# The first batch's softmax divided after the value product: sums from products with ones, in a fused attention and two-FFN kernel

## The chip, the cores and the metric

The kernel runs on one core of a Trainium2 chip. The metric is the device time of one execution in microseconds (us); lower is better. Inputs and outputs are float32 in the chip's main memory.

## What is computed

Three layers, one after the other:

```
attn:  4 batches, 8 heads, 576 positions, 64 columns a head
       scores = q k^T / 8, masked; heads 0-3: a local window (0 <= rel < 32),
       heads 4-7: positions with the same remainder by 32, causal
       e = exp(scores - max);  attn = e / (sum(e) + 1e-9);  out = attn v
x = out as [2304 tokens, 512]
moe:   xn = x / sqrt(mean(x*x) + 1e-6) * rms_g
       y = (silu(xn w_gate) * (xn w_val)) w_out        (512 -> 1536 -> 512)
moe2:  the same without the norm, with weights of its own
```

## The kernel before

**Numbers.** A product of the FFN layers is done on values split into a high and a low part (type fp32r), as three products. The weights are split on the chip: per half megabyte of weights a `weight_step` (line 311) has `low` and `high` on ScalarE (L288, L280), `sign` and `join` on VectorE (L292, L297), then a cast on ScalarE (L305) and a subtraction on VectorE (L309). The products of the attention are plain float32.

**Stages.** Attention is cut into batches. The first batch (`b` = 0) runs alone, ahead of all FFN work (`state["start"]` is true, lines 1134 to 1143); beside it only the first weights are loaded and split. When the first columns of `x` are normed (L887), they are split (L1000, L1001) and the products of the first FFN layer begin. Batches 1 to 3 run in the gaps of that layer. From about a fifth of the run on only FFN work is left.

**One batch** has ten groups: five of strided heads (tiles of 126 or 108 rows) and five of local heads (tiles of 128 queries by 96 keys; the last has half as many). A group has four (the last two) score tiles and goes through three steps, each a list of phases:

- `softmax_step` (line 663): `pe`, the score products on TensorE into one or two banks of PSUM; `top`, on VectorE the mask, the scale and the row minimum (L677); `exp`, on ScalarE one exponential a tile, which also accumulates the row's sum (L686, `accum_out`; the profile shows each as an ACTIVATE and an ACTIVATION_READ_ACCUMULATOR); `norm`, on VectorE sum + 1e-9 and a reciprocal of one column a tile (L696, L697), on GpSimd one multiplication of the group's tiles (L703).
- `turn_step` (line 712): four transposes on TensorE, one copy out of PSUM on ScalarE (`pT`).
- `local_v` / `strided_v` (lines 754, 799): the product with v into a bank `op` of 512 columns, of which 256 or fewer are used, and copies from there into `x` (L87 on ScalarE; in the first two strided groups also a piece of 36 columns on VectorE, L89).

After groups 4, 6 and 9 `squares` (line 828) adds up x squared; `rms_step` (line 849) makes the norm's factor and applies it.

**Order.** `point()` moves every active step on by one phase and starts at most one new one; the list made by `batch` (line 903) puts group i's scores before the transposes of group i-3 and the value product of group i-4. TensorE's order in the first batch is fixed by that list (`traced`, line 53). On the other engines a planner orders what is ready, attention ahead of weight work (`PRIO_W`). Seven banks of PSUM go round among the first batch's steps; the eighth takes the constant products.

**Constant products.** In the first batch `keep_busy` (line 67) puts products of a constant 128x128 by 128x256 (`att.warm`, L72), whose result nobody reads, ahead of chosen groups of products; the number of each place is in a table.

Of the kernel before, what the change touches and what calls it, by code (L numbers as in the profile page):

```python
# [15 lines left out]
DRAM = bass.MemoryType.DRAM  # L16

NEG = -8.0e9
PRIO = 200
PRIO_A = 400  # L20
PRIO_R = 1500
# [4 lines left out]
def attn_ffn_ffn(ctx: ExitStack, tc: tile.TileContext, q, k, v, w1g, w1v, w1o, rms_g, w2g, w2v, w2o, out):  # L26
# [40 lines left out]
    def keep_busy():  # L67
        if state["start"] and state["kind"] and state["group"] != state["filled"]:
            state["filled"] = state["group"]
            state["count"] += 1  # L70
            for _ in range({1: 26, 11: 34, 14: 16, 20: 6, 27: 8, 28: 5, 31: 7, 34: 9, 36: 22, 40: 2, 43: 5}.get(state["count"], 0)):
                traced(nc.tensor.matmul(att.fill, att.warm[:, :128], att.warm, start=True, stop=True))  # L72

    def product(out_, a, b_, start, stop, **how):
# [420 lines left out]
    class Attention:  # L495
        def __init__(self, actx):
            cp = actx.enter_context(tc.tile_pool(name="cp", bufs=1))
            self.p1 = actx.enter_context(tc.tile_pool(name="p1", bufs=1))
            self.p2 = actx.enter_context(tc.tile_pool(name="p2", bufs=2))
            self.ident = cp.tile([128, 128], F32, name="ident")  # L500
            self.ones = cp.tile([128, 128], F32, name="ones")
            self.warm = cp.tile([128, 256], F32R, name="warm")
            self.fill = bank("v")[:, :256]
            self.m0 = cp.tile([128, 96], F32, name="m0")
            self.m1 = cp.tile([128, 96], F32, name="m1")
            self.ms = cp.tile([128, 128], F32, name="ms")[:, 0:126]
            self.gcol = cp.tile([128, 32], F32, name="gcol")[:, 0:KC]
            self.expo = cp.tile([128, 32], F32, name="expo")
            self.ld = {}
            self.vt = {}  # L510
            self.qk = {}
            self.st = {}
            self.x = {}
            self.ss = {}
            self.done = set()
            self.sq = set()
            self.turned = {}
            self.nbank = 0
            self.tags = ["a0", "a1", "g", "y0", "y1", "y2", "y3"]
            self.turn = 0  # L520
# [10 lines left out]
        def consts(self):  # L531
            g = nc.gpsimd

            def sel(t, pattern, base, cm, op=ALU.is_ge, fill=NEG):
                g.affine_select(out=t, in_=t, pattern=pattern, compare_op=op, fill=fill, base=base, channel_multiplier=cm)

            row = self.ms[0:7]
            g.memset(row, 0.0)
            sel(row[:, 0:108].rearrange("p (t a) -> p t a", a=6), [[0, 18], [-1, 6]], 0, 1, ALU.not_equal, 1.0)
            sel(row[:, 108:126], [[0, 18]], -6, 1, ALU.not_equal, 1.0)  # L540
            same = bank("g")
            nc.tensor.matmul(same[0:126, 0:126], row, row, start=True, stop=True)
            nc.vector.tensor_scalar(out=self.ms[0:126], in0=same[0:126, 0:126], scalar1=1.0, scalar2=-NEG, op0=ALU.subtract, op1=ALU.mult)
            for m, leads in ((self.m0, (0, 32)), (self.m1, (32, 32))):
                g.memset(m, 0.0)
                for par, lead in enumerate(leads):
                    sel(m[64 * par:64 * par + 64], [[-1, 96]], lead, 1)
                    sel(m[64 * par:64 * par + 64], [[1, 96]], 31 - lead, -1)
            sel(self.ms[0:126], [[-1, 126]], 0, 1)
            g.memset(self.expo, -0.5)  # L550
            nc.sync.dma_start(out=self.gcol, in_=rms_g.rearrange("(c p) -> p c", p=128))

        def load_strided(self, t, src, b, eng):
# [109 lines left out]
        def softmax_step(self, ready, key, qn, kn, mks, mms):  # L663

            cell = {}
            nt = len(mks)

            def pe():
                cell["s"] = mms()

            def top():
                sp = cell["s"]
                cell["e"] = e = self.p2.tile([128, 4, 128], F32, tag="e", name="e", bufs=6)
                cell["nb"] = nb = self.p2.tile([128, 32], F32, tag="nb", name="nb", bufs=6)
                for i, mk in sorted(enumerate(mks), key=lambda im: im[0] % 2):

                    r = nc.vector.tensor_tensor_reduce(out=e[:qn, i, :kn], in0=sp[i], in1=mk[:qn, :kn], scale=-0.125,  # L677
                                                       scalar=3.0e38, op0=ALU.add, op1=ALU.min, accum_out=nb[:qn, i:i + 1])
                if state["start"]:
                    last["dve"] = ins_of(r)  # L680

            def exp():
                e, nb = cell["e"], cell["nb"]
                cell["sums"] = sums = self.p2.tile([128, 32], F32, tag="sums", name="sums", bufs=6)
                for i in range(nt):
                    r = nc.scalar.activation(out=e[:qn, i, :kn], in_=e[:qn, i, :kn], func=AF.Exp, bias=nb[:qn, i:i + 1],  # L686
                                             scale=-1.0, accum_out=sums[:qn, i:i + 1])
                if state["start"]:
                    last["act"] = ins_of(r)

            def norm():
                e, sums = cell["e"], cell["sums"]
                rc = self.p2.tile([128, 32], F32, tag="rc", name="rc", bufs=6)
                self.nnorm = getattr(self, "nnorm", -1) + 1
                eng = nc.gpsimd
                nc.vector.tensor_scalar(out=sums[:qn, :nt], in0=sums[:qn, :nt], scalar1=1e-9, scalar2=None, op0=ALU.add)  # L696
                nc.vector.reciprocal(out=rc[:qn, :nt], in_=sums[:qn, :nt])  # L697
                if eng is None:
                    for i in range(nt):
                        nc.vector.tensor_scalar(out=e[:qn, i, :kn], in0=e[:qn, i, :kn], scalar1=rc[:qn, i:i + 1], scalar2=None,  # L700
                                                op0=ALU.mult)
                if eng is not None:
                    eng.tensor_tensor(out=e[:qn, :nt, :kn], in0=e[:qn, :nt, :kn], in1=rc[:qn, :nt].unsqueeze(2).to_broadcast([qn, nt, kn]), op=ALU.mult)  # L703
                if key[1] == 0 or not 3:
                    self.st[key] = e

            def put():
                self.st[key] = cell["e"]

            return Step([pe, top, exp, norm] + ([wait] * (3 - 1) + [put] if 3 and key[1] else []), ready, kind="s")  # L710

        def turn_step(self, key, qn, kn, nt):
            cell = {}
# [40 lines left out]
        def local_v(self, b, tiles, last):  # L754
            cell = {}

            def pe():
                cell["o"] = op = self.abank()
                vt = self.vt[b, 0]
                pT = self.st.pop(("T", ("l", b, tiles)))  # L760
                n = 0
                for i, halves in enumerate(tiles):
                    for par, (pair, j) in enumerate(halves):
                        for hp in range(2):
                            product(op[64 * hp:64 * hp + 64, 64 * n:64 * n + 64], vt[:, 2 * pair + hp, j, :],
                                    pT[:96, 2 * i + hp, 64 * par:64 * par + 64], start=True, stop=True)
                        n += 1

            def post():
                x = self.x_tile(b, 0)  # L770
                p0, j0 = tiles[0][0]
                if j0 == NW - 1:
                    copy(self.eng(), x[:, :, 64 * j0:S], cell["o"][:, 0:128].rearrange("p (a k) -> p a k", a=2))
                else:
                    copy(self.eng(), x[:, p0, 64 * j0:64 * (j0 + 4)], cell["o"][:, 0:256])

            return Step([pe, post] + ([lambda: self.squares(b, last)] if last else []),
                        lambda: ("T", ("l", b, tiles)) in self.st, kind="v")
# [20 lines left out]
        def strided_v(self, b, part, pair):  # L799
# [4 lines left out]
            def pe():  # L804
# [3 lines left out]
                for k in range(2):  # L808
                    for hp in range(2):
                        i = 2 * k + hp if pair is None else 2 * hp + k  # L810
                        gi, h = subs[i]
                        g = 2 * part + gi
                        product(op[64 * hp:64 * hp + 64, 128 * k:128 * k + n], vt[:n, h, g * D:(g + 1) * D], pT[:n, i, :n], start=True, stop=True)

            def post():
                x = self.x_tile(b, 1)
                for k in range(2):
                    g = 2 * part + k if pair is not None else 4
                    d = x[:, k if pair is None else pair].rearrange("p (t r) -> p t r", r=32)
# [908 lines left out]
```

## Time and profile before

| | |
|---|---|
| median of 3 runs | 997.48 us (997.15 to 999.68) |
| profiled execution, own time | 1001.4 us |
| its span | 999.5 us |
| busy: TensorE / weight loads / VectorE / ScalarE / GpSimd | 969.5 / 892.3 / 582.3 / 577.7 / 385.3 us |
| mean granted TensorE clock | 0.995 |

The busy shares are averages over stages that differ. The change touches the first batch alone, the stretch up to about 52 us; after 70 us TensorE is busy nearly all the time. So what counts is how long the opening takes and what the engines still owe when it ends.

### The profile page before, as it was taken

Reading aid. Unit: us, or ns where it says so; the run is one execution under the profiler, and the core shown is the slowest. Engines: PE = TensorE matmul, PEld = TensorE weight load, DVE = VectorE, ACT = ScalarE, POOL = GpSimd, SP = SyncE. Lnnn points to the kernel's source line nnn. Section 1 sums busy time; section 2 is a strip of 40 time slices with the busy share of each in tenths; the row PEclk is TensorE's granted clock in tenths of the full one; section 3 lists DMA queues with packets and bytes.
Section 4 is the critical chain, followed back from the end, with each engine's and each line's share of the span. In section 5 each row is a group of like instructions: output and inputs, shape, how many; then the busy total and the mean of one; then the engine's idle time right before and its main releaser. Section 6 shows DMA issues by size and latency. Waiting matters only on the chain.

```text
span 999.5 us, 17788 instructions
## 1 busy us (share of the span) xinstructions
PE 969.5 (97%) x6054; PEld 892.3 (89%) x6054; DVE 582.3 (58%) x1319; ACT 577.7 (58%) x1465; POOL 385.3 (39%) x416
## 2 busy tenths in 40 slices
PE   8889998999999999999999999999999999999998
PEld 8778866777989999899999998999999999899997
DVE  5796768867335656456645646545557554563334
ACT  6998776864335645456554556554656546553431
POOL 3221244621221628152535556571616334341500
PEclk9999999999999999999999999999999999999999
DMA  7884558848684766996758685556978396865211
GB/s 195 230 218 149 155 176 255 260 161 304 208 293 153 216 195 196 317 297 205 248 190 288 238 261 209 177 199 250 316 263 260 117 348 218 292 208 164 88 61 64
DMA packets 168455, 215.89 MB, mean 216 GB/s; under 512 B 46860, under 2 KB 122028, under 8 KB 168364
## 3 DMA queue, kind: packets, MB, share of 16 engines
q1 hardware_dynamic: 158559, 199.48, 61.8%
q10 hardware_dynamic: 9805, 15.27, 4.2%
q8 instruction: 48, 0.79, 0.3%
q14 instruction: 43, 0.35, 0.1%
HBM read 142.87 MB, written 71.83 MB: 215 GB/s over the span
## 4 chain that ended last, share of the span: by engine, by line
PE 79%; DMA 8%; ACT 6%; DVE 4%; issue 2%; SPq 1%; POOL 0%; ACTq 0%; DVEq 0%; POOLq 0%
PE b_y L76 33%; PE b_a L76 17%; PE b_g L76 14%; PE b_v L76 13%; DMA raw<-in_moe_w_out_dram 2%; PE b_y L80 2%; DMA pk<-raw 1%; ACT e L686 1%; DMA part<-ob 1%; PE b_a L80 1%; SPq L160 1%; ACT raw L288 1%; ACT dh L280 1%; DVE dh L297 1%; DMA ob<-part 1%
## 5 line engine op out<-in xcount | busy, mean ns | idle before, releaser
L1401 POOL TENSOR_TENSOR xl<-xst,xh 128x384 fp32r<-128x384 f32 x196 | 210.7, 1096 | 181.5 <-ACT xh L1400 61.8
L76 PE MATMUL b_y<-xh,w 128*128 128x384 f32 (+1 forms) x800 | 215.3, 334 | 2.5 <-ACT t L1458 2.1
L76 PEld LDWEIGHTS b_y<-xh,w 128*128 128x128 f32 x800 | 145.7, 188 | 5.5 <-ACT t L1458 2.7
L76 PE MATMUL b_a<-xh,w 128*128 128x384 f32 (+2 forms) x512 | 141.6, 336 | 3.0 <-ACT t L1458 3.0
L76 PE MATMUL b_y<-xl,w 128*128 128x384 f32 (+1 forms) x400 | 133.6, 334 | 0.0
L76 PE MATMUL b_g<-xh,w 128*128 128x384 f32 (+2 forms) x408 | 125.6, 349 | 0.3 <-DVE w L309 0.3
L76 PE MATMUL b_v<-xh,w 128*128 128x384 f32 (+2 forms) x344 | 105.9, 351 | 1.3 <-ACT t L1472 1.3
L76 PEld LDWEIGHTS b_a<-xh,w 128*128 128x128 f32 x512 | 93.2, 188 | 7.0 <-ACT t L1458 4.7
L1400 ACT CAST xh<-xst 128x384 fp32r<-128x384 f32 x196 | 91.6, 520 | 0.0
L386 POOL TENSOR_TENSOR raw<-dh 128x256 f32<-128x256 f32 x40 | 29.6, 757 | 153.1 <-DVE dh L297 55.5
L76 PE MATMUL b_a<-xl,w 128*128 128x384 f32 (+2 forms) x256 | 85.9, 335 | 0.0
L76 PE MATMUL b_y<-hh,w 128*128 128x384 f32 (+2 forms) x304 | 81.2, 341 | 0.0
L76 PEld LDWEIGHTS b_g<-xh,w 128*128 128x128 f32 x408 | 75.5, 190 | 5.7 <-DVE w L309 0.5
L76 PEld LDWEIGHTS b_y<-xl,w 128*128 128x128 f32 x400 | 75.1, 188 | 1.8
L76 PEld LDWEIGHTS b_v<-xh,w 128*128 128x128 f32 x344 | 63.6, 190 | 6.6 <-ACT t L1472 1.6
L76 PE MATMUL b_g<-xl,w 128*128 128x384 f32 (+2 forms) x204 | 69.2, 339 | 0.0
L703 POOL TENSOR_TENSOR e<-e,rc 128x384 f32<-128x384 f32 (+3 forms) x40 | 37.1, 932 | 79.1 <-DVE rc L697 19.8
L76 PE MATMUL b_y<-w,hh 128*128 128x512 f32 x216 | 67.1, 391 | 0.0
L686 ACT ACTIVATE e<-e,nb 128x96 f32<-128x96 f32 (+2 forms) x152 | 57.1, 382 | 4.6 <-DVE nb L677 4.3
L76 PE MATMUL b_v<-xl,w 128*128 128x384 f32 (+2 forms) x172 | 58.7, 341 | 0.0
L76 PEld LDWEIGHTS b_y<-hh,w 128*128 128x128 f32 x304 | 54.8, 188 | 3.1 <-issue 0.2
L1478 DVE TENSOR_TENSOR b_y<-b_y,t 128x384 f32<-128x384 f32 x56 | 31.7, 566 | 42.4 <-ACT b_y L1472 41.5
(216 smaller groups left out, 2152.8 us busy)
## 6 DMA issues: line engine op xcount, KB each, us to landing
w<-pk SPq DMA_DIRECT2D x48, 512.0 KB
raw<-in_moe_w_gate_dram SPq DMA_DIRECT2D x24, 512.0 KB
raw<-in_moe_w_val_dram SPq DMA_DIRECT2D x24, 512.0 KB
raw<-in_moe_w_out_dram SPq DMA_DIRECT2D x24, 512.0 KB
pk<-raw ACTq DMA_DIRECT2D x48, 256.0 KB
part<-ob SPq DMA_DIRECT2D x48, 256.0 KB
xst<-y_d SPq DMA_DIRECT2D x30, 384.0 KB
xst<-xq SPq DMA_DIRECT2D x28, 384.0 KB
```

Source lines behind the costliest of these rows:

```text
L76: traced(nc.tensor.matmul(out_, a, b_, start=start, stop=stop, **how))
L80: traced(nc.tensor.transpose(out_, a, one))
L160: nc.sync.dma_start(out=out, in_=in_)
L280: nc.scalar.activation(out=cell["h"], in_=cell["hw"].bitcast(F32), func=AF.Copy, scale=2.0 ** -112)
L288: nc.scalar.activation(out=cell["r"], in_=cell["lw"], func=AF.Copy, scale=LOW)
L297: nc.vector.scalar_tensor_tensor(out=h, in0=h, scalar=3, in1=cell["r"], op0=ALU.logical_shift_left, op1=ALU.bitwise_or)
L386: paced(nc.gpsimd.tensor_tensor(out=t[:, z], in0=a, in1=b, op=ALU.subtract))
L686: r = nc.scalar.activation(out=e[:qn, i, :kn], in_=e[:qn, i, :kn], func=AF.Exp, bias=nb[:qn, i:i + 1], scale=-1.0, accum_out=sums[:qn, i:i ...
L703: eng.tensor_tensor(out=e[:qn, :nt, :kn], in0=e[:qn, :nt, :kn], in1=rc[:qn, :nt].unsqueeze(2).to_broadcast([qn, nt, kn]), op=ALU.mult)
L1400: nc.scalar.copy(out=xh[:, kk], in_=src[:, kk])
L1401: paced(nc.gpsimd.tensor_tensor(out=xl[:, kk], in0=src[:, kk], in1=xh[:, kk].bitcast(F32), op=ALU.subtract), ("pe", None))
L1478: nc.vector.tensor_tensor(out=s, in0=s, in1=v, op=ALU.mult)
```

## The change

In the first batch, and there alone (`key[1]` or `b` is 0):

- The exponentials don't accumulate sums, and the `norm` phase is gone: raw exponentials are transposed and multiplied with v.
- After the value product of a group, `sums_of` writes the row sums into the other half of the same bank: one product of three constant rows (`tiny` by `warm`, which gives the 1e-9) and, for each of the two halves of the partitions, one float32 product of ones with the group's transposed tiles (256 columns; 252 or 216 in strided groups; half in the last group).
- `inverse` takes, on VectorE, the reciprocal of those sums (all of them: each query has its sum in 64 partitions) into a tile of `e`; then VectorE multiplies the value product by it on the way into `x`, in place of ScalarE's copies: one multiplication in a local group, two in a strided one, three in the first two.
- The table of constant products has 54 fewer, of 114 that come after the first one's 26.
- Three small GpSimd instructions and one VectorE copy make `tiny` at the start.

```diff
@@ -16,6 +16,7 @@
 DRAM = bass.MemoryType.DRAM
 
 NEG = -8.0e9
+EPS = (137 * 2.0 ** -37, 56 * 2.0 ** -44, 95 * 2.0 ** -53)
 PRIO = 200
 PRIO_A = 400
 PRIO_R = 1500
@@ -68,7 +69,7 @@
         if state["start"] and state["kind"] and state["group"] != state["filled"]:
             state["filled"] = state["group"]
             state["count"] += 1
-            for _ in range({1: 26, 11: 34, 14: 16, 20: 6, 27: 8, 28: 5, 31: 7, 34: 9, 36: 22, 40: 2, 43: 5}.get(state["count"], 0)):
+            for _ in range({1: 26, 11: 20, 14: 10, 20: 3, 27: 4, 28: 2, 31: 3, 34: 4, 36: 8, 40: 1, 43: 5}.get(state["count"], 0)):
                 traced(nc.tensor.matmul(att.fill, att.warm[:, :128], att.warm, start=True, stop=True))
 
     def product(out_, a, b_, start, stop, **how):
@@ -505,6 +506,7 @@
             self.m1 = cp.tile([128, 96], F32, name="m1")
             self.ms = cp.tile([128, 128], F32, name="ms")[:, 0:126]
             self.gcol = cp.tile([128, 32], F32, name="gcol")[:, 0:KC]
+            self.tiny = cp.tile([128, 128], F32R, name="tiny")[0:3]
             self.expo = cp.tile([128, 32], F32, name="expo")
             self.ld = {}
             self.vt = {}
@@ -548,6 +550,11 @@
                     sel(m[64 * par:64 * par + 64], [[1, 96]], 31 - lead, -1)
             sel(self.ms[0:126], [[-1, 126]], 0, 1)
             g.memset(self.expo, -0.5)
+            eps = self.p2.tile([128, 32], F32, tag="nb", name="eps", bufs=6)[0:3]
+            g.memset(eps, EPS[0])
+            sel(eps, [[0, 32]], 0, -1, fill=EPS[1])
+            sel(eps, [[0, 32]], 1, -1, fill=EPS[2])
+            nc.vector.tensor_copy(out=self.tiny.rearrange("p (a k) -> p a k", a=4), in_=eps.unsqueeze(1).to_broadcast([3, 4, 32]))
             nc.sync.dma_start(out=self.gcol, in_=rms_g.rearrange("(c p) -> p c", p=128))
 
         def load_strided(self, t, src, b, eng):
@@ -681,33 +688,42 @@
 
             def exp():
                 e, nb = cell["e"], cell["nb"]
+                if not key[1]:
+                    for i in range(nt):
+                        r = nc.scalar.activation(out=e[:qn, i, :kn], in_=e[:qn, i, :kn], func=AF.Exp, bias=nb[:qn, i:i + 1], scale=-1.0)
+                    last["act"] = ins_of(r)
+                    self.st[key] = e
+                    return
                 cell["sums"] = sums = self.p2.tile([128, 32], F32, tag="sums", name="sums", bufs=6)
                 for i in range(nt):
-                    r = nc.scalar.activation(out=e[:qn, i, :kn], in_=e[:qn, i, :kn], func=AF.Exp, bias=nb[:qn, i:i + 1],
-                                             scale=-1.0, accum_out=sums[:qn, i:i + 1])
-                if state["start"]:
-                    last["act"] = ins_of(r)
+                    nc.scalar.activation(out=e[:qn, i, :kn], in_=e[:qn, i, :kn], func=AF.Exp, bias=nb[:qn, i:i + 1],
+                                         scale=-1.0, accum_out=sums[:qn, i:i + 1])
 
             def norm():
                 e, sums = cell["e"], cell["sums"]
                 rc = self.p2.tile([128, 32], F32, tag="rc", name="rc", bufs=6)
-                self.nnorm = getattr(self, "nnorm", -1) + 1
-                eng = nc.gpsimd
                 nc.vector.tensor_scalar(out=sums[:qn, :nt], in0=sums[:qn, :nt], scalar1=1e-9, scalar2=None, op0=ALU.add)
                 nc.vector.reciprocal(out=rc[:qn, :nt], in_=sums[:qn, :nt])
-                if eng is None:
-                    for i in range(nt):
-                        nc.vector.tensor_scalar(out=e[:qn, i, :kn], in0=e[:qn, i, :kn], scalar1=rc[:qn, i:i + 1], scalar2=None,
-                                                op0=ALU.mult)
-                if eng is not None:
-                    eng.tensor_tensor(out=e[:qn, :nt, :kn], in0=e[:qn, :nt, :kn], in1=rc[:qn, :nt].unsqueeze(2).to_broadcast([qn, nt, kn]), op=ALU.mult)
-                if key[1] == 0 or not 3:
-                    self.st[key] = e
+                nc.gpsimd.tensor_tensor(out=e[:qn, :nt, :kn], in0=e[:qn, :nt, :kn], in1=rc[:qn, :nt].unsqueeze(2).to_broadcast([qn, nt, kn]), op=ALU.mult)
 
             def put():
                 self.st[key] = cell["e"]
 
-            return Step([pe, top, exp, norm] + ([wait] * (3 - 1) + [put] if 3 and key[1] else []), ready, kind="s")
+            return Step([pe, top, exp] + ([norm, wait, wait, put] if key[1] else []), ready, kind="s")
+
+        def sums_of(self, out_, n, parts_):
+
+            k, w = parts_[0].shape[1:]
+            out_ = out_.rearrange("p (k m) -> p k m", k=2)[:, :k, :w]
+            product(out_, self.tiny, self.warm[0:3, 0:k * w].rearrange("p (k m) -> p k m", k=k), start=True, stop=True)
+            for hp, p in enumerate(parts_):
+                product(out_[64 * hp:64 * hp + 64], self.ones[:n, 0:64], p, start=False, stop=True, skip_group_check=True)
+
+        def inverse(self, op, k, w):
+            o, t = (t[:, 256 * i:256 * i + 256].rearrange("p (k m) -> p k m", k=2)[:, :k, :w] for i in range(2) for t in (op,))
+            r = self.p2.tile([128, 4, 128], F32, tag="e", name="rs", bufs=6)[:, :k, :w]
+            nc.vector.reciprocal(out=r, in_=t)
+            return o, r
 
         def turn_step(self, key, qn, kn, nt):
             cell = {}
@@ -765,11 +781,20 @@
                             product(op[64 * hp:64 * hp + 64, 64 * n:64 * n + 64], vt[:, 2 * pair + hp, j, :],
                                     pT[:96, 2 * i + hp, 64 * par:64 * par + 64], start=True, stop=True)
                         n += 1
+                if not b:
+                    self.sums_of(op[:, 256:512], 96, [pT[:96, hp:2 * len(tiles):2] for hp in range(2)])
 
             def post():
                 x = self.x_tile(b, 0)
                 p0, j0 = tiles[0][0]
-                if j0 == NW - 1:
+                if not b:
+                    o, r = self.inverse(cell["o"], len(tiles), 128)
+                    if j0 == NW - 1:
+                        d, o, r = x[:, :, 64 * j0:S], o[:, 0].rearrange("p (a k) -> p a k", a=2), r[:, 0].rearrange("p (a k) -> p a k", a=2)
+                    else:
+                        d = x[:, p0, 64 * j0:64 * (j0 + 4)].rearrange("p (k m) -> p k m", k=2)
+                    nc.vector.tensor_tensor(out=d, in0=o, in1=r, op=ALU.mult)
+                elif j0 == NW - 1:
                     copy(self.eng(), x[:, :, 64 * j0:S], cell["o"][:, 0:128].rearrange("p (a k) -> p a k", a=2))
                 else:
                     copy(self.eng(), x[:, p0, 64 * j0:64 * (j0 + 4)], cell["o"][:, 0:256])
@@ -811,9 +836,21 @@
                         gi, h = subs[i]
                         g = 2 * part + gi
                         product(op[64 * hp:64 * hp + 64, 128 * k:128 * k + n], vt[:n, h, g * D:(g + 1) * D], pT[:n, i, :n], start=True, stop=True)
+                if not b:
+                    self.sums_of(op[:, 256:512], n, [pT[:n, hp::2, :n] if pair is None else pT[:n, 2 * hp:2 * hp + 2, :n] for hp in range(2)])
 
             def post():
                 x = self.x_tile(b, 1)
+                if not b:
+                    o, r = self.inverse(cell["o"], 2, n)
+                    for k in range(2):
+                        g = 2 * part + k if pair is not None else 4
+                        d = x[:, k if pair is None else pair].rearrange("p (t r) -> p t r", r=32)
+                        nc.vector.tensor_tensor(out=d[:, :, g:g + 26:5], in0=o[:, k, 0:108].rearrange("p (t r) -> p t r", r=6),
+                                                in1=r[:, k, 0:108].rearrange("p (t r) -> p t r", r=6), op=ALU.mult)
+                    if part == 0:
+                        nc.vector.tensor_tensor(out=d[:, :, 30:32].rearrange("p t r -> p r t"), in0=o[:, :, 108:126], in1=r[:, :, 108:126], op=ALU.mult)
+                    return
                 for k in range(2):
                     g = 2 * part + k if pair is not None else 4
                     d = x[:, k if pair is None else pair].rearrange("p (t r) -> p t r", r=32)
```

## Rows read from the trace of the kernel before

**Rows 1.** Stretches: us; PE, PEld, DVE, ACT, POOL busy; clock, DMA share, GB/s.

```profile
11.40:49.20 37.80, 33.86 (x403) 29.76 (x400) 28.99 (x128) 35.76 (x131) 10.62 (x12) 1.00 0.82 229
...
49.20:70.00 20.80, 16.56 (x140) 13.96 (x138) 20.18 (x85) 19.69 (x69) 5.50 (x6) 1.00 0.87 232
70.00:100.00 30.00, 29.69 (x348) 26.04 (x347) 20.80 (x84) 25.87 (x92) 4.94 (x6) 1.00 0.49 150
```

**Rows 2.** Chain that ended last, 20 to 52 us: shares by line.

```profile
by line: ACT e L686 24.4%; ACT dh L280 8.8%; ACT raw L288 8.6%; ACT pT L87 8.5%; ACT w L305 7.8%; ACT x L87 7.6%; PE b_y L80 4.6%; ACT xh L1000 4.1%; PE b_g L76 4.0%; PE b_y L76 3.7%; PE b_v L72 3.2%; ACT qT L87 3.0%; ACT kT L87 3.0%; PE b_
```

**Rows 3.** Waits of TensorE, 11.4 to 49.2 us: us in total, times, longest.

```profile
PE b_g L76 <- ACT pT L87: 1.9, 2, 1.4
PE b_y L80 <- POOL e L703: 1.0, 1, 1.0
PE b_y L76 <- ACT pT L87: 0.5, 1, 0.5
```

**Rows 4.** ScalarE in order of time: start us, duration us, what.

```profile
15.16 0.37 ACT L686 ACTIVATE e<-e,nb 108x108 f32<-108x108 f32 x1
...
15.53 0.37 ACT L686 ACTIVATE e<-e,nb 108x108 f32<-108x108 f32 x1
...
38.47 0.38 ACT L87 COPY x<-b_y 128x108 f32<-128x108 f32 x1
38.59 0.42 ACT L686 ACTIVATE e<-e,nb 128x96 f32<-128x96 f32 x1
```

**Rows 5.** The stretch again: VectorE busy (count) with line 696, then 697, alone.

```profile
11.40:49.20 37.80, 3.26 (x10) 1.00 0.82 229
...
11.40:49.20 37.80, 1.76 (x10) 1.00 0.82 229
```

**Rows 6.** VectorE by line and form, same stretch: busy us, mean ns, idle before.

```profile
L697 DVE RECIPROCAL rc<-sums 128x4 f32<-128x4 f32 x4 | 0.7, 178 | 0.1
...
L89 DVE COPY x<-b_y 128x36 f32<-128x36 f32 x2 | 0.5, 230 | 0.1
...
L697 DVE RECIPROCAL rc<-sums 128x2 f32<-128x2 f32 x1 | 0.2, 166 | 0.0
```

**Rows 7.** VectorE in order of time: start us, duration us, what.

```profile
14.27 0.17 DVE L697 RECIPROCAL rc<-sums 126x4 f32<-126x4 f32 x1
14.35 0.24 DVE L677 CUSTOM_DVE_ANT_0 e<-b_y,ms 108x108 f32<-108x108 f32 x1
...
49.16 1.65 DVE L887 SCALAR_TENSOR_TENSOR x<-x,gcol,b_g 128x256 f32<-128x256 f32 x4
```

**Rows 8.** VectorE by line and form, whole run: one line in two lengths.

```profile
L1562 DVE TENSOR_TENSOR ob<-ob,b_y 128x384 f32<-128x384 f32 x24 | 12.7, 550 | 3.4 <-PE b_y L76 3.3
L1562 DVE TENSOR_TENSOR ob<-ob,b_y 128x512 f32<-128x512 f32 x18 | 12.2, 686 | 8.8 <-PE b_y L76 8.8
```

**Rows 9.** TensorE in order of time; a float32 product is two records.

```profile
12.49 4.34 PE L72 MATMUL b_v<-warm 128*128 128x256 f32 x34
...
21.19 0.65 PE L76 MATMUL b_y<-pT,vs 126*64 126x126 f32 x8 [0.49 <-ACT pT L87]
21.77 0.66 PE L80 MATMUL b_y<-ident,qn 128*128 128x128 f32 x4
...
52.03 0.36 PE L76 MATMUL b_g<-xh,w 128*128 128x256 f32 x1
```

**Rows 10.** Stretches as in rows 1: two empty ones of TensorE, and after.

```profile
62.00:64.00 2.00, 0.30 (x3) 0.10 (x1) 2.00 (x14) 2.00 (x11) 1.00 (x1) 1.00 0.80 203
64.00:66.00 2.00, 1.53 (x13) 1.40 (x14) 1.97 (x8) 2.00 (x11) 0.41 (x1) 1.00 0.93 290
...
126.00:128.00 2.00, 0.00 (x0) 0.00 (x0) 1.90 (x3) 1.77 (x5) 0.85 (x1) 1.00 0.42 151
128.00:130.00 2.00, 1.77 (x7) 0.97 (x7) 0.99 (x3) 0.27 (x1) 0.00 (x0) 0.70 0.26 66
130.00:132.00 2.00, 2.00 (x23) 1.50 (x24) 1.71 (x10) 1.17 (x3) 0.41 (x1) 0.50 0.43 109
```

## The prediction

> **What bounds the kernel now.** I read the page's busy times first, then the run by stretches. From 70 us on TensorE is busy 29.69 of 30 us [rows 1], so the change, which touches the first batch alone, matters through the length of the opening, which shifts all that follows. In the opening, from 11.4 us (the first score tile reaches VectorE) to 49.2 us (the first normed columns of x) ScalarE is busy 35.76 of 37.8 us, TensorE 33.86, VectorE 28.99 [rows 1]. The chain of waits runs over ScalarE there: the exponentials alone are a quarter of it [rows 2]. TensorE's 33.86 us are no need of its own: 114 constant products fill it, and its waits for copies by ScalarE and for GpSimd's division come on top, 3.4 us in all [rows 3]. So ScalarE sets the opening, and VectorE has 8.8 us to spare. In the next stretch, to 70 us, VectorE is busy 20.18 of 20.8 us and ScalarE 19.69, while TensorE has only 16.56: what VectorE still owes at 49 us is not made good before 70.
>
> **What the change takes away.** ScalarE: 38 exponentials start 0.37 us apart with the sum's read-out between them; a copy of 108 columns without one lets the next start after 0.12 us [rows 4]. I take 0.15 us, since the exponentials read SBUF: 38 x 0.22 = 8.4 us (bounds: 0, if the distance is the exponential's own, and 9.5). The copies into x: ten of 0.12 us and, by the same time a column, four of 0.28 and one of 0.14, 2.5 us. ScalarE falls to 35.8 - 10.9 = 24.9 us and no longer sets anything. GpSimd loses ten multiplications, and every group the way over VectorE and GpSimd between exponential and transposes; of TensorE's waits only 1.0 us hung on GpSimd [rows 3]. VectorE loses ten additions (3.3 us busy, much of it waiting), ten reciprocals of two or four columns (1.8 us) [rows 5] and two copies of 36 columns (0.5 us) [rows 6]: 5.6 us.
>
> **What it adds on TensorE.** 54 constant products fewer at 4.34 / 34 = 0.128 us are 6.9 us [rows 9]. The sums: four float32 products of 126 columns in alternate halves of the partitions take 21.77 - 21.19 = 0.58 us, 0.145 each [rows 9]; one of 256 columns then takes 0.29 us, two 0.59, and the constant rows 0.13 as one constant product: 0.72 us for a group of 256 columns, 0.70 and 0.62 for 252 and 216, 0.36 for the last. Over ten groups: 4 x 0.72 + 2 x 0.70 + 3 x 0.62 + 0.36 = 6.5 us. TensorE breaks even (-0.4 us; the products with ones are 5.3 us of it, so -3.1 if they take half of that, +4.9 if twice).
>
> **What it adds on VectorE.** This decides. The reciprocal is no longer of four columns but of every sum in 64 partitions: 4 x 256 + 128 + 2 x 252 + 3 x 216 = 2304 columns in all. The trace has it only small: 178 ns for four columns, 166 for two [rows 6], so 6 ns a column over some 154 ns fixed. From below: other instructions of VectorE pay (686 - 550) / 128 = 1.06 ns a column [rows 8]. From above: if the engine takes two columns at a time from SBUF but one from PSUM, the 12 ns between the rows belong to one column. I take 6 ns, the slope that the instruction itself shows: 2304 x 6 = 13.8 us, and 10 x 0.154 = 1.5 us fixed, of which 0.09 us each overlaps with the next (14.27 to 14.35 [rows 7]): 14.4 us. Ends: 3.0 us and 28.2 us.
>
> In the Trainium skill, the page "VectorE: DVE Perf Modes" (section "First, the fixed hardware budget") speaks against this edit: reciprocal is an iterative divide on the slices with a repeat count of eight, where plain operations give an element a cycle. Eight cycles of that page's 0.96 GHz would be 8.3 ns, an estimate; the sum would be 19.2 in place of 13.8 us. The trace agrees with the kind, at 6 ns [rows 6], not with the size.
>
> The multiplications read PSUM like the norm's scaling, of which four of 256 columns take 1.65 us [rows 7], 0.41 each; less 1.06 ns a column, one of 108 takes 0.25, of 36 0.17, of 128 0.27: 4 x 0.41 + 0.27 + 10 x 0.25 + 2 x 0.17 = 4.8 us. Added together: 19.2 us.
>
> VectorE's need in the stretch: 29.0 - 5.6 + 19.2 = 42.6 us, where there were 37.8: 4.8 us over, if it never idled. It will idle a little: it cannot start before the first scores, and the last group ends in a reciprocal and a multiplication one after the other (about 1.2 us, against one copy of 0.3) before the second part's squares. I add 0.7 us. The weight work on VectorE ranks behind the attention and could slip past 49 us, but the next 20 us have 0.6 us free [rows 1], so a slip only moves the debt. Behind a long reciprocal on VectorE stand the next group's `top` instructions, for which ScalarE and then TensorE wait, and the bank of the value product comes free 2 us after it is full, not 0.3; with seven banks in turn that alone holds nothing up. In TensorE's queue the norm's first product waits for `squares`, and those now for VectorE.
>
> The constant for 1e-9 (three GpSimd instructions and a copy at the start) hides behind the first loads; uncovered it would cost under 1 us.
>
> **The sum.** 1001.4 us of the profiled execution + 4.8 + 0.7 = 1006.9. The profiled execution lies 3.9 us above the median of the runs (997.48), which is what is compared: 997.5 + 5.5 = 1003.0 us.
>
> **Rivals.**
> - *Reciprocals as quick as other instructions.* Place: the ten `inverse` calls. At 1.06 ns a column VectorE needs 42.6 - 11.4 = 31.2 of 37.8 us and sets nothing; TensorE's waits (3.4 us [rows 3]) go, its products save 0.4, and the longer tail costs 0.3: -3.5, 994.0 us. It decides at the rate where VectorE's need is just 37.8 us: 6 - 4.8 / 2.304 = 3.9 ns a column. For it: only counts of two and four are in the trace, and a start-up may hide there. Against it: both are the same start-up, and their difference is a slope. Chance 0.18.
> - *The debt is absorbed.* After 70 us VectorE has 9.2 of 30 us free [rows 1]. If weight work needed late is put off until there, and ScalarE's 11 us let the rest run ahead, the opening's end moves by under 2 us: some 998.5 us. Against it: the layer that starts at 52 us needs those weights at once. Chance 0.18.
> - *Reciprocals dearer still.* Between 8 and 12 ns a column VectorE owes 4.6 to 13.8 us more: 1007.6 to 1016.8, about 1009 for the lower half. The page named above would give 1008. Chance 0.12.
> - *The clock falls.* An empty stretch of over 2 us at 126 to 128 us was followed by a granted clock of 0.70 and then 0.50 (the lower level, 1.2 GHz), one of about the same length at 62 to 64 us by none [rows 10]. With half the constant products gone, a wait for VectorE leaves TensorE empty; 4 us at half the clock cost 2 us. This rides on the forecast (1005) rather than beside it.
> - *The change doesn't do what it says*: exponentials still start 0.37 us apart without the read-out. ScalarE then keeps 33.3 us, VectorE is still the longer one, and the time is that of the forecast.
>
> **How the numbers follow.** The forecast, VectorE the bound at 5 to 7 ns, has 0.52; its own range is 999 to 1008. A measurement of this kernel tells 0.3%, 3 us, from no change. Faster by more: most of the first rival and a little of the second, 0.18. Within it: most of the second rival, a piece of the first and the forecast's low end, 0.21. Slower: the rest, 0.61. The range 994 to 1010 leaves out half of the first rival, when TensorE gains more than I count, and the dearest reciprocals.
>
> **What would show it.** In the changed profile: RECIPROCAL rows of 256 columns of about 1.7 us (0.4 us proves the first rival, over 2.2 the third); exponentials starting about 0.15 us apart, with no read-out rows in the first batch; VectorE near full from 25 us on, ScalarE under 27 us before the first norm; TensorE waiting for VectorE (`top`, the bank of x, `squares`) where it waited for `pT`; and the first product of the FFN layer 4 to 7 us after the 52.03 us of before [rows 9]. If that product comes at or before 52 us with VectorE full, my step from VectorE's load to the opening's length is wrong.

## The result and the profile after

The kernel after takes 1013.46 us (median of four runs, 1012.03 to 1016.61), the one before 998.58 beside it: 1.0138 times as long, 95% interval [1.0112, 1.0163]. The forecast was 1003.0 us in a range of 994 to 1010: slower was right, and so was the engine, but the loss is 14.9 us where I expected 5.5. The profiled execution of after spans 1011.7 us.

The loss is made in the opening. The first product of the FFN layer, at 52.03 us before [rows 9], now starts 16.7 us later (TensorE in order of time):

```profile
68.72 0.36 PE L77 MATMUL b_g<-xh,w 128*128 128x256 f32 x1
```

The opening of after by stretches, columns as in [rows 1]; the first row reaches to the first scaling of x by the norm, as 11.4 to 49.2 did before:

```profile
11.40:63.60 52.20, 44.77 (x398) 33.56 (x395) 40.26 (x130) 30.31 (x77) 0.83 (x2) 0.80 0.64 171
...
11.40:30.00 18.60, 16.77 (x151) 13.07 (x151) 13.51 (x64) 16.30 (x43) 0.00 (x0) 0.88 1.00 249
30.00:45.00 15.00, 12.13 (x140) 8.79 (x136) 14.97 (x49) 9.49 (x24) 0.00 (x0) 0.84 0.87 256
45.00:57.00 12.00, 9.28 (x76) 6.41 (x72) 8.23 (x12) 4.37 (x11) 0.00 (x0) 0.78 0.04 13
57.00:64.00 7.00, 7.00 (x48) 5.70 (x49) 3.92 (x8) 0.55 (x2) 0.83 (x2) 0.50 0.23 54
```

VectorE's column is the one to read. It has 40.26 us of work (the forecast counted 42.6), and yet the stretch lasts 52.2: it idles 11.9 us. It is full from 30 to 45 us only, and 6.0 of these 15 us are weight steps, which rank behind the attention. Before that few value products are there to divide (the first two reciprocals start at 21.35 and 29.86 us); after it a chain goes round the engines, and VectorE is busy 8.23 of 12 us and then 3.92 of 7.

That chain, VectorE in order of time (in brackets the idle time and what ended it):

```profile
51.09 1.76 DVE L725 RECIPROCAL rs<-b_g 128x256 f32<-128x256 f32 x1 [0.91 <-PE b_g L77]
53.17 1.76 DVE L725 RECIPROCAL rs<-b_y 128x256 f32<-128x256 f32 x1 [0.33 <-PE b_y L77]
54.85 0.36 DVE L796 TENSOR_TENSOR x<-b_g,rs 128x256 f32<-128x256 f32 x1
55.13 0.41 DVE L796 TENSOR_TENSOR x<-b_y,rs 128x256 f32<-128x256 f32 x1
55.75 0.42 DVE L883 TENSOR_TENSOR ss<-ss,sq 128x256 f32<-128x256 f32 x1 [0.21 <-ACT sq L882]
57.35 0.16 DVE L905 TENSOR_SCALAR mean<-b_y 128x2 f32<-128x2 f32 x1 [1.17 <-PE b_y L77]
59.96 1.76 DVE L725 RECIPROCAL rs<-b_a 128x256 f32<-128x256 f32 x1 [2.46 <-PE b_a L77]
61.64 0.38 DVE L913 TENSOR_SCALAR dg<-ident,rstd 128x128 f32<-128x128 f32 x2
61.94 0.95 DVE L725 RECIPROCAL rs<-b_a 128x128 f32<-128x128 f32 x1
```

Three of these four reciprocals wait for TensorE; ScalarE's squares wait for x; VectorE adds the squares; TensorE's column product waits for these, and idles 2.72 us; and the norm's diagonal (`dg`), for which GpSimd has the factor ready at 58.30 us, starts at 61.64, behind one more reciprocal. The waits of ScalarE and of TensorE in 11.4 to 63.6 us (total, times, longest) say the same; of [rows 3] GpSimd has gone, ScalarE's copies are still there, and VectorE has come:

```profile
ACT sq L882 <- DVE x L796: 13.4, 3, 7.0
ACT e L693 <- DVE nb L684: 5.5, 6, 1.3
```

```profile
PE b_y L77 <- DVE ss L883: 2.7, 1, 2.7
PE b_y L81 <- DVE nb L684: 2.0, 1, 2.0
PE b_y L77 <- ACT pT L88: 1.6, 2, 0.8
```

The prices, VectorE by line and form in the same stretch (busy us, mean ns, idle before), against the small reciprocals of [rows 6]:

```profile
L725 DVE RECIPROCAL rs<-b_a 128x256 f32<-128x256 f32 x2 | 3.5, 1754 | 2.5 <-PE b_a L77 2.5
...
L725 DVE RECIPROCAL rs<-b_a 128x128 f32<-128x128 f32 x1 | 0.9, 949 | 0.0
```

128 columns more cost 805 ns, 6.3 ns a column. By the shapes, four of 1756, two of 1730, three of 1493 and one of 949 ns, the ten are 15.9 us, where the forecast's durations came to 15.3 before overlap.

And TensorE around one group's sums, and the wait that follows the last fill:

```profile
51.55 0.69 PE L77 MATMUL b_y<-pT,vl 96*64 96x64 f32 x16
52.16 0.38 PE L77 MATMUL b_y<-warm,tiny 3*128 3x256 f32 x1
52.47 0.65 PE L77 MATMUL b_y<-pT,ones 96*64 96x256 f32 x4
53.06 0.42 PE L81 MATMUL b_y<-ident,e 128*96 128x128 f32 x2
53.24 0.36 PE L73 MATMUL b_v<-warm 128*128 128x256 f32 x1
56.32 0.98 PE L77 MATMUL b_y<-ones,ss 128*128 128x1 f32 x4 [2.72 <-DVE ss L883]
```

From 52.16 to 53.06 us a group's sums take 0.90 us (constant rows 0.31, products with ones 0.59), where I had counted 0.72.

### The profile page after: what moved, and what is told of

It is laid out like the page before. It is cut to its first block, busy times and chain, and to the rows that moved or that the text cites. A ratio compares the mean times of both kernels' runs of the same rounds, so it can differ in the third digit from the quotient of the medians.

```text
span 1011.7 us, 17706 instructions
## 1 busy us (share of the span) xinstructions
PE 982.5 (97%) x6050; PEld 898.6 (89%) x6050; DVE 593.0 (59%) x1325; ACT 573.1 (57%) x1412; POOL 377.6 (37%) x409
## 4 chain that ended last, share of the span: by engine, by line
PE 86%; DVE 4%; DMA 3%; ACT 3%; issue 1%; SPq 1%; POOL 0%; DVEq 0%; POOLq 0%; ACTq 0%
PE b_y L77 37%; PE b_a L77 18%; PE b_g L77 15%; PE b_v L77 13%; PE b_y L81 2%; PE b_a L81 1%; DMA qn<-in_q_dram 1%; DMA pk<-dh 1%; DVE rs L725 1%; DMA part<-ob 1%; DVE raw L293 0%; DMA raw<-in_moe_w_gate_dram 0%; ACT e L693 0%; DVE dh L298 0%; DMA xst<-xq 0%
## 5 line engine op out<-in xcount | busy, mean ns | idle before, releaser
L293 DVE SCALAR_TENSOR_TENSOR raw<-raw 128x512 uint32<-128x512 uint32 x55 | 48.0, 875 | 12.2 <-ACT raw L289 11.9
L1495 ACT COPY t<-b_y 128x384 f32<-128x384 f32 x56 | 27.1, 483 | 47.1 <-PE b_y L77 44.8
```

What stands on the lines that cost most here:

```text
L293: nc.vector.scalar_tensor_tensor(out=cell["r"], in0=cell["hw"], scalar=0x80000000, in1=cell["r"], op0=ALU.bitwise_and, op1=ALU.bitwise_or)
L1495: last["act"] = ins_of(nc.scalar.copy(out=t, in_=self.x[:, :HN]))
```

## The experiments

Four theories were tried. **Load**: the reciprocals' time on VectorE, which executes in order. **Chain**: their place between the value product and x, squares and mean. **Clock**: too few constant products, so that TensorE's granted clock falls. **Other parts**: sums, removal, multiplications. Two marks are read in each run: the first product of the local values (before 37.97 us, after 44.13) and the first product of the FFN layer (52.03 and 68.72). In the quoted texts A, B and C are named anew in each; what each stands for is said there. Runs of before on the chips used had medians of 1001.0 to 1001.7 us; every ratio is against those on the same chip.

**e1_fills: after with the old table.**

```
-for _ in range({1: 26, 11: 20, 14: 10, 20: 3, ... 36: 8, 40: 1, 43: 5}...
+for _ in range({1: 26, 11: 34, 14: 16, 20: 6, ... 36: 22, 40: 2, 43: 5}...
```

> The changed kernel with the old table of constant products (54 more). Theory A, the clock: most of the 14.9 us are TensorE at the lower level (about 20 us of the opening at 0.50, worth some 10 us), and the constant products were what kept it up; then about 1004 us, clock 1.0 up to 54 us, first FFN product near 59 us in place of 68.7. Theory B, VectorE: the reciprocals set the opening by themselves, through what they stand in front of; then TensorE's extra 6.9 us lie in waits, and the time stays at 1011 to 1015. The forecast as it stood (VectorE's load, 5.5 us over) would want 1003 to 1005 here.

Measured: 1.0151 [1.0114, 1.0189]; FFN at 66.90 us. The granted clock (third number from the end) is full up to 54 us here, and the opening is still 14.9 us longer than before's:

```profile
30.00:45.00 15.00, 12.85 (x148) 9.49 (x147) 14.55 (x50) 10.45 (x27) 0.00 (x0) 1.00 0.79 222
45.00:54.00 9.00, 6.89 (x73) 5.21 (x72) 7.55 (x10) 2.33 (x6) 0.00 (x0) 1.00 0.22 61
54.00:66.00 12.00, 10.59 (x67) 8.98 (x68) 8.10 (x19) 5.00 (x13) 0.84 (x2) 0.57 0.39 99
```

Too few constant products are not the cause: the full table brings back 1.8 us of the opening, and nothing that the total shows. The clock itself stays in play, though. Here as in after it is at 0.50, the lower level, at the end of the opening (55 to 64 us here), behind a wait in which TensorE is empty for 2.60 us, and no run with all these reciprocals keeps it up there.

**e2_copy: after, the reciprocal replaced by a copy of the same shape.**

```
-nc.vector.reciprocal(out=r, in_=t)
+nc.vector.tensor_copy(out=r, in_=t)
```

> The changed kernel with each reciprocal replaced by a copy of the same columns, out of PSUM into the same tile (0.42 in place of 1.75 us for 256 columns; the output is multiplied by the sums, not divided). VectorE has 11 us less. Theory A: the clock still falls, since the table is the short one: about 1008 us, with stretches at 0.50 before 60 us. Theory B: the time falls to 996 to 1000, about the kernel before. The forecast's first rival (cheap reciprocals) said 994.

Measured: 1.0047 [1.0030, 1.0064]; local values at 41.05, FFN at 56.96 us. A copy of 256 columns takes 0.42 us, so ten copies in place of the ten reciprocals leave VectorE some 12 us less, and the FFN product comes 11.8 us earlier. The total lies between the two expectations. Where after had VectorE full:

```profile
30.00:45.00 15.00, 12.25 (x129) 8.93 (x125) 10.54 (x41) 10.49 (x27) 0.00 (x0) 0.89 0.81 241
```

**e3_fills_copy: both edits.**

> Both: the old table and copies in place of reciprocals (output not divided). Theory A and theory B together, if the two add up: e1's gain plus e2's. If they feed each other (a wait for VectorE empties TensorE, the clock falls, the products come later), this one is near e2: 996 to 1000. If TensorE is then the bound, its 6.5 us of sums on top of the full table show: 1001 to 1004.

Measured: 1.0031 [1.0009, 1.0054]; FFN at 57.01 us. TensorE has no gap left from 11.4 to 45 us, and VectorE has. Yet e2, with 54 constant products fewer and gaps on TensorE, opens as early (56.96), so TensorE's work alone is not shown to be the bound:

```profile
11.40:30.00 18.60, 18.60 (x195) 15.47 (x192) 14.13 (x76) 17.17 (x46) 0.00 (x0) 1.00 0.99 252
30.00:45.00 15.00, 15.00 (x177) 12.03 (x173) 11.39 (x43) 10.84 (x28) 0.00 (x0) 1.00 0.91 248
```

**e4_before_few: before with the new table.** The edit of e1 the other way round.

> The kernel before with the new, shorter table of constant products, nothing else. Theory A: with 54 fewer constant products TensorE waits on ScalarE instead, is emptier, and the clock falls to 0.50 somewhere in the opening: 1001 to 1006 us. Theory B: ScalarE sets this opening, so the time stays at 998 +- 1 and the clock at 1.0.

Measured: 0.9993 [0.9974, 1.0012]; FFN at 53.76 us. Fewer constant products alone cost nothing in all. The opening ends 1.7 us later, and the granted clock is 0.50 from 45 to 51 us, where theory B had it at 1.0.

**g1_remove and g2_sums: the removal alone, then with the sums, old table.** In g1 the four `if not b:` of the value steps (sums, division) become `if False:`; in g2 only the two of the division.

> Only what the change removes: the exponentials of the first batch leave no sums and the scaling of the exponentials on POOL with its two VectorE steps is gone; no products with ones, ScalarE copies to x as before, the old table of constant products. The output of the first batch is not divided. Theory A (my forecast's sum: what is removed was hidden but for some 3 us of TensorE's waits): the exponentials 0.28 us apart save 3 to 4 us of ScalarE, the first FFN product starts at 49 to 52 us where before's was at 52, ratio 0.995 to 1.000. Rival B (a step less per group moves the order of the groups and costs by itself): the first FFN product later than 53 us, ratio over 1.002.

> The kernel of the removal with the change's products for the sums added; nobody reads the sums, ScalarE copies to x, the output of the first batch is not divided. Theory A (with the old table TensorE is the bound of the opening, 10 groups of 0.85 to 0.9 us): the first FFN product 6 to 9 us later than in the removal alone, at 56 to 58 us, the ratio 1.002 to 1.005, the same as with the copy in place of the reciprocal (1.003): then the multiplications on VectorE cost nothing. Rival B (the forecast's: the sums go where TensorE waited): under 3 us later, ratio under 1.001, and what the copies and multiplications on VectorE add is then the rest.

Measured: 1.0063 [1.0039, 1.0088] and 1.0118 [1.0089, 1.0148], FFN at 59.56 and 63.85 us: g1 in rival B's range, g2's ratio above both of its ranges, and for a reason that none of them names. The generated order of SP's queue had put the last part of the local values behind the next batch's q and k. SP's queue in g1 (start, duration, what):

```profile
37.84 0.54 SPq L161 DMA_DIRECT2D raw<-in_moe_w_val_dram  x1
38.42 0.50 SPq L598 DMA_DIRECT2D vl<-in_v_dram  x1
```

and TensorE there:

```profile
44.82 1.12 PE L77 MATMUL b_a<-pT,vl 96*64 96x64 f32 x16 [7.86 <-DMA vl<-in_v_dram]
```

In after nobody waits for that load, which SP's queue issues ten us earlier:

```profile
28.43 0.45 SPq L598 DMA_DIRECT2D vl<-in_v_dram  x1
28.98 0.34 SPq L562 DMA_DIRECT2D qn<-in_q_dram  x1
```

Both runs thus say nothing of the change's parts, but something of what a displaced load costs here. They were made again with that load held ahead of the next batch's.

**h1_remove and h2_sums: the same with the order mended.**

```
+    if b == 1:
+        for r in rs:                      # strided loads of the next batch
+            follow(ins_of(r), done_["vl", 0])   # issue order alone
```

> The removal alone once more (first batch: no sums of the exponentials, no scaling by POOL, no products with ones, ScalarE copies to x, old table; output of that batch not divided), with the last part of the local values ordered ahead of the loads of the next batch on SP's queue; in the first such run it was issued at 38.4 us instead of 28 and TensorE waited 7.9 us for it. Theory A (that wait was the whole loss; what is removed was all but hidden): the first local value product at 36 to 38 us, the first FFN product at 50 to 52 us, ratio 0.996 to 1.000. Rival B (one step less per group costs by itself): the first FFN product at 54 us or later, ratio over 1.002.

> The same with the products for the sums, which nobody reads, and the same order of the loads. Theory A (TensorE is the bound with the old table, some 0.87 us for each of 10 groups): the first local value product 2 to 4 us and the first FFN product 5 to 8 us later than in the removal alone, ratio 1.002 to 1.006; as the copy in place of the reciprocal gave 1.003, VectorE's multiplications then cost nothing. Rival B: under 3 us later, ratio under 1.001.

Measured: h1 0.9997 [0.9979, 1.0015], local values at 36.34, FFN at 49.94 us. h2 1.0060 [1.0042, 1.0077], 40.19 and 57.07 us. The removal gives 2.1 us of the opening, and no measurable time in all; the sums, with the full table, take 7.1 us of it. TensorE in h2 is without a gap, as in e3:

```profile
11.40:30.00 18.60, 18.60 (x198) 15.77 (x198) 12.22 (x67) 17.76 (x49) 0.00 (x0) 1.00 1.00 250
30.00:45.00 15.00, 15.00 (x170) 11.84 (x166) 9.25 (x35) 12.99 (x39) 0.00 (x0) 1.00 0.74 223
```

e3 differs from h2 by copies and multiplications on VectorE in place of ScalarE's copies into x, and opens as early (57.01): this costs nothing there. Its lower total is not read: the two ran on different chips, and the intervals overlap.

**g3_order: after, each reciprocal ordered behind the last group's multiplication.**

```
-nc.vector.reciprocal(out=r, in_=t)
+ri = ins_of(nc.vector.reciprocal(out=r, in_=t))
+if "mul" in done_: follow(ri, done_["mul"])
```

> After with each reciprocal held behind the multiplication of the group before it on VectorE (in after two of them ran ahead of it). Theory A (the order: the reciprocal that ran ahead held x, the squares and the mean by some 2 us): the first FFN product 2 to 4 us earlier than after's 68.7, ratio 1.009 to 1.012. Theory B (the load and place of the reciprocals, in whatever order they run): the first FFN product within 1.5 us of 68.7, ratio 1.012 to 1.016.

Measured: 1.0126 [1.0102, 1.0149]; FFN at 66.28 us, 2.4 earlier than after's, as theory A had it; the ratio lies in theory B's range, and its interval covers after's. The order is worth at most 2.4 us of the opening, and nothing that the total shows.

**g4_beside: before, with ten idle reciprocals of the same shapes.**

```
+r = self.p2.tile([128, 4, 128], F32, tag="e", ...)[:, :2, :w]
+nc.vector.reciprocal(out=r, in_=self.ones[:, :w]...to_broadcast([128, 2, w]))
```

> Before, unchanged in what it computes, with ten reciprocals of after's shapes (some 16 us of VectorE) put behind the copies to x of the first batch; they read a constant, write a scratch tile and nobody waits for them but VectorE itself. Theory A (the chain: in after each reciprocal stands between the value product and x, and so the squares and the mean wait for it; off that chain VectorE has 8.8 us to spare in the stretch): first FFN product at 52 to 57 us, ratio 1.000 to 1.004. Theory B (the sum of VectorE's work as the forecast made it, 29.0 + 16 against 37.8 us): about 59 to 60 us, ratio 1.005 to 1.008. Theory C (VectorE executes in order and every reciprocal delays the chain wherever it stands): 64 us and later, ratio 1.010 and more.

Measured: 1.0083 [1.0059, 1.0108]; local values at 42.90, FFN at 61.18 us. Nobody reads these reciprocals, and they still move the opening by 9.2 us, as VectorE takes them in order between its other steps. Theory A falls: load alone delays an opening. B is nearest, and both numbers lie a little beyond its ranges. The same stretch and the price, from a constant in SBUF:

```profile
30.00:45.00 15.00, 10.96 (x105) 9.20 (x105) 14.50 (x45) 13.57 (x53) 1.77 (x3) 0.77 0.70 209
```

```profile
L714 DVE RECIPROCAL rs<-ones 128x256 f32<-128x256 f32 x4 | 7.0, 1746 | 0.0
```

It is not after's delay over again, though. Among the steps that the reciprocals hold back are the row sums that before still has on VectorE, and with them GpSimd's scaling. TensorE waits 5.1 us for that scaling, where it waited 1.0 [rows 3]; after has no such path:

```profile
36.29 1.09 PE L80 MATMUL b_g<-ident,e 128*96 128x128 f32 x4 [2.63 <-POOL e L703]
...
46.10 1.09 PE L80 MATMUL b_a<-ident,e 128*96 128x128 f32 x4 [2.51 <-POOL e L703]
```

**h3_local and h4_strided: the change in one kind of group.** The other kind keeps sums from the exponentials, GpSimd's scaling and copies.

```
-if not key[1]:
+if (key[1], key[0]) == (0, "l"):      # h4: "s"
```

> The change in the local groups alone (five reciprocals of 128x256 or 128x128, 7.9 us of VectorE, at the end of the opening); the strided groups as before; table of after. Theory A (the place: from the first local value product on the reciprocals stand one behind the other between TensorE and x, the squares and the mean): the first local value product at 37 to 40 us (before 38.0), from there to the first FFN product 20 to 24 us (before 14.1, after 24.6), ratio 1.006 to 1.010. Theory B (VectorE's load alone): it has room there, under 17 us, ratio under 1.003.

> The change in the strided groups alone (five reciprocals of 128x252 or 128x216, 7.9 us of VectorE, between 19 and 44 us); the local groups as before; table of after. Theory B (VectorE's load: it is full from 30 to 45 us in after and holds the masking of the local scores back): the first local value product at 41 to 44 us (before 38.0, after 44.1), from there to the first FFN product 14 to 16 us as before, ratio 1.004 to 1.007. Theory A (only the place at the end counts): the first local value product by 40 us, ratio under 1.003.

Measured: h3 1.0051 [1.0033, 1.0070], local values at 36.20, FFN at 59.72 us: 23.5 us between the marks, as theory A said, where before had 14.1; the first mark and the ratio are a little under its ranges. h4 1.0054 [1.0035, 1.0073], 43.99 and 57.45 us: the whole delay comes before the first mark, and the 13.5 us after it are before's. VectorE is the third number of busy time; the first two rows are h3's and the next two h4's:

```profile
30.00:45.00 15.00, 11.28 (x137) 8.15 (x137) 11.80 (x35) 12.40 (x36) 0.00 (x0) 1.00 0.79 224
45.00:57.00 12.00, 8.70 (x62) 7.07 (x61) 9.90 (x21) 4.71 (x13) 0.83 (x2) 0.72 0.49 131
```

```profile
30.00:45.00 15.00, 12.85 (x122) 9.23 (x120) 14.37 (x50) 9.78 (x34) 3.48 (x4) 0.73 0.85 246
45.00:57.00 12.00, 9.88 (x117) 8.91 (x114) 7.64 (x28) 9.85 (x28) 1.34 (x3) 0.95 0.30 77
```

With the strided reciprocals VectorE is full from 30 to 45 us; the local ones lengthen the end. Alone they move the opening by 7.7 and 5.4 us, together by 16.7, so 3.6 us appear only with both. How much of h3's longer end is the chain itself? Between the marks it takes 9.5 us more than before. With reciprocals that nobody waits for it was 4.2 more (g4: 61.18 - 42.90 = 18.3), and the sums alone bring 3.3 (h2 16.9 against h1 13.6). If these add, about 2 us are left for the place in the chain. That is a subtraction of single executions, and g4's 4.2 us hold one of the two waits for GpSimd (2.5 us), which h3's local groups don't have; so the chain's share is not settled, and may be larger.

**The opening as a ladder** (start of the first FFN product, one profiled execution each, and the ratio of the total):

| kernel | FFN us | step | ratio to before |
|---|---|---|---|
| before | 52.03 | | 1 |
| h1: removal | 49.94 | -2.1 | 0.9997 |
| h2: + sums on TensorE | 57.07 | +7.1 | 1.0060 |
| e3: + copies and multiplications on VectorE for ScalarE's copies | 57.01 | -0.1 | 1.0031 |
| e1: + reciprocals | 66.90 | +9.9 | 1.0151 |
| after: + short table | 68.72 | +1.8 | 1.0138 |

The steps hold for this order of the parts, and the ratios come from several chips.

**Where the 9.9 us arise.** e1 and e3 differ in the reciprocals alone, for which e3 has copies. 3.6 us come before the first local value product (39.32 and 42.93 us), 6.3 between the marks. TensorE there in e3, then in e1:

```profile
48.11 0.50 PE L77 MATMUL b_y<-ones,ss 128*128 128x1 f32 x4
48.55 0.69 PE L77 MATMUL b_a<-pT,vl 96*64 96x64 f32 x16
...
49.96 0.40 PE L77 MATMUL b_a<-pT,vl 96*64 96x64 f32 x8
...
51.60 0.61 PE L77 MATMUL b_g<-dg,ones 128*128 128x128 f32 x4
```

```profile
54.49 0.99 PE L77 MATMUL b_y<-ones,ss 128*128 128x1 f32 x4 [2.60 <-DVE ss L883]
55.41 1.12 PE L77 MATMUL b_a<-pT,vl 96*64 96x64 f32 x16
...
57.88 0.64 PE L77 MATMUL b_a<-pT,vl 96*64 96x64 f32 x8
...
60.71 1.05 PE L77 MATMUL b_g<-dg,ones 128*128 128x128 f32 x4
```

Up to the norm's column product (`ones,ss`) e1 takes 2.8 us more than e3, from there to the product of the norm's diagonal 2.7 more (6.2 against 3.5), and to the FFN product 0.8. In the middle part the column product and the next group's value product and sums take 3.39 us, at a granted clock that falls to 0.50, and 1.85 in e3 at full clock. So about 1.5 us of it are the lower level behind TensorE's wait; the rest goes with the reciprocal in front of `dg`. How the 6.3 us divide between plain order, chain and clock beyond that is open.

## Why the prediction was wrong

- **Which engine**: right in the main. VectorE's reciprocals are the largest step, 9.9 of 16.7 us, with what the lower clock behind them costs.
- **The reciprocal's price**: right, 6.3 ns a column where I took 6. The rival of quick reciprocals, which I gave 0.18, falls, and so does that of dearer ones. The Trainium skill's page "VectorE: DVE Perf Modes" (section "First, the fixed hardware budget") gives the reciprocal a repeat count of eight, which at that page's 0.96 GHz would be 8.3 ns, an estimate. The rows agree with the kind, at 6.3 ns, and not with the size.
- **VectorE's need**: right, 40.3 us against 42.6.
- **From that need to the length of the stretch**: here the forecast failed. "I add 0.7 us" for idling; it was 11.9 (52.20 - 40.26). I spread the work evenly over the stretch, and it can't be spread: a reciprocal can only run when its value product is there. Up to 30 us only two are, and VectorE idles 5.1 of 18.6 us; then the rest of the strided ones, with the weight steps, keep it full for 15 us and hold back the masking of the local scores (local values 6.2 us later, 3.6 of it by the reciprocals: e1 against e3); then the local ones meet the squares and the mean, each of which goes round over TensorE, ScalarE or GpSimd and back, and VectorE idles 6.8 us of the last 18.6. "The last group ends in a reciprocal and a multiplication one after the other" saw one group of this tail; all five lie in it. g4 shows that plain order, VectorE's other steps standing behind each 1.75 us, can delay an opening by 9.2 us, in part on a path that after lacks; how much of after's delay is order and how much the chain to x is not shown. The engine that the sum named as the bound is full in less than a third of the opening.
- **TensorE breaks even**: the second step that failed, by about 5 us: with the sums and cheap copies for the reciprocals the opening already ends 5.0 us later than before's (e3, and e2 with the short table). The sums cost 0.90 us a group of 256 columns, not 0.72: the products with ones are 0.59 as worked out, but the three constant rows take 0.31, not 0.13. And the constant products saved don't pay for them: the short table alone gained nothing (e4), the sums move the opening by 7.1 us (h2).
- **ScalarE -10.9 us**: too much. With the read-out gone 16 exponentials take 4.65 us, 0.29 each and not 0.15; 38 save 3 us. ScalarE is busy 30.31 us up to the first scaling, not 24.9. It cost the forecast little, since ScalarE no longer bounds, and the removal as a whole brings no measurable time (h1).

```profile
12.01 4.65 ACT L693 ACTIVATE e<-e,nb 126x126 f32<-126x126 f32 x16 [0.29 <-DVE nb L684]
```

- **The clock**: it fell, as that rival allowed, in several stretches, and last to 0.50 from 57 us on, behind the empty 2.72 us. The earlier falls, which the full table takes away, are worth no more than the 1.8 us between e1 and after. The last one stands in both; it is worth about 1.5 us in the part that e1 and e3 compare, and what it costs in all is not shown.
- **The debt absorbed after 70 us**: for the smaller part at most. Of the opening's 16.7 us, 12.2 remain between the two profiled spans, and 14.9 between the medians.

## What to carry to other kernels

An engine's work, added up over a stretch, is only a lower bound of its length: ask when the first and the last of it can start. Work put between two products of TensorE can run only where the values come, and what an in-order engine already does there waits behind it, even if nobody reads the result. When a part of a change is tried alone, look first whether the queues still issue their loads in the same order: here one displaced load cost 7.9 us of waiting and would have been taken for the part's own price.

## What was not expected of the hardware

- The reciprocal costs the same from PSUM (1754 ns for 256 columns) as from a constant in SBUF (1746): its price is its own, not the source's.
- The exponential's read-out of its sum adds only 0.08 us to the distance between two (0.37 [rows 4] against 0.29).
- A product over three partitions and 256 columns takes 0.31 us at full clock, half of two products over 96 partitions with the same columns together (0.59), and over twice a constant product of 256 (0.128 [rows 9]). With 128 columns it takes 0.25 us (e3, 50.29 to 50.54), so most of its time does not go with the columns. Why stays open.
